# Moving layer one's twelve integer adds from VectorE to GpSimd, and ten early score products from ScalarE and GpSimd to VectorE

## The chip, the cores and the metric

The kernel runs on one core of a Trainium2 chip. The metric is device time in microseconds (us) for one execution; lower is better. A core has TensorE (PE in the profile; its weight loads are PEld), VectorE (DVE), ScalarE (ACT), GpSimd (POOL) and SyncE (SP), which here issues all DMA transfers. Each engine works through its own queue in order and waits on semaphores for the others.

## What is computed

The reference runs a chunked linear attention and then two feed-forward layers over its 3072 rows, all in fp32:

```python
# attention, per batch and head, chunk by chunk (768 positions, head_dim 32, d_state 16)
cum = np.cumsum(la, axis=-1)                          # la = log(clip(a))
L = np.exp(cum[..., :, None] - cum[..., None, :]) * causal
M = np.einsum('bhin,bhjn->bhij', Cc, Bc) * L          # scores times decays
y = einsum(M, xc) + einsum(Cc, state) * np.exp(cum)
state = decay_full * state + sum(Bx * decay_from_j)
...
# layer one: d_model 256, d_ff 768
h = np.maximum(np.maximum(x @ w1, x @ w2), x @ w3);  x = h @ w_out
# layer two: d_model 256, d_ff 1536
gate = 1 / (1 + exp(-(x @ w_gate)));  x = (gate * (x @ w_val)) @ w_out
```

The weights of both layers arrive as 64-bit floats, seen as pairs of 32-bit words, so the kernel itself turns them into fp32 and splits each into a high and a low part. Every large product is then three matmuls: low times high, high times low, high times high.

## The kernel before

**Attention.** There are 64 steps k, 8 for each of 8 chunks of 96 positions. A step makes scores on TensorE into a PSUM tile `s` (L331 for the first 16 steps, in fp32; L334 later, in bf16). It multiplies them by the decays `dec` into the SBUF tile `mt`, and TensorE multiplies `mt` with `xs` into `y` (L352). Which engine forms the product depends on k: odd steps, and all of the first four, use one VectorE multiply straight from PSUM (L346); even steps from k = 4 on use a ScalarE copy out of PSUM (L342) and then a GpSimd multiply in SBUF (L343), since GpSimd here works only on SBUF. In every step GpSimd writes a further 64 columns of `mt` (L339). `mt` is a ring of five buffers. `dec` tiles, one for two steps, are a ring of four: SyncE loads the next (L268) once the products that read an old one are done, and VectorE scans it (L290, twice a tile). After every fourth step ScalarE and VectorE split `y` into `xt_hi` and `xt_lo` (L361, L363) and VectorE transposes the state into the next chunk's `xs` (L367).

**Layer one's weights.** They come as 12 pieces, `a00`, `a01`, `a10`, ... `a51`: a block m of 128 hidden columns has a piece m0 (first two up matrices) and m1 (third up matrix, and the down matrix). SyncE loads a piece (L149), some of them queued behind a `dec` load. Decoding it takes these instructions, each over 128 x 512 words: ScalarE L164, L169, L173; VectorE L177 (shift and or into `t_a`); VectorE L182, the exact 32-bit integer add into `r_a`, which appears in the profile as a custom operation over 128 x 1024 halves of 16 bits; ScalarE L210 (the high part of `w_a`); GpSimd L212 (the low part of `w_a`). Layer two's weights go through the same function later, with the add on VectorE too.

**Feed-forward.** The 3072 rows are 6 tiles of 512. For a tile and a block m, TensorE makes three `u` tiles of six matmuls each (L401 to L403), and the larger of the three is taken by a ScalarE copy (L469) and two VectorE operations (L471, L473); ScalarE and GpSimd split it (L462, L464), and six matmuls into `o` follow. `u_0_5_0` is tile 0, block 5, first matrix. All `s` and `u` tiles share one ring of three PSUM buffers (`psu`), so a `u` or an `s` can start only when the tile three before it has been read out. Attention steps 12 to 23 are woven into tile 0.

**Order.** Python code emits the steps through small pipelines, and a scheduler then sets the order on each engine; so an edit moves rows elsewhere too.

```python
            dve.tensor_tensor(out=r, in0=t, in1=r, op=ALU.add)          # L182, in decode()
...
        if k >= 4 and k % 2 == 0:                                        # L341, in attention()
```

Of the kernel before, what the change touches and what calls it, by code (L numbers as in the profile page):

```python
# [15 lines left out]
ALU = mybir.AluOpType  # L16
# [25 lines left out]
START = 12  # L42
FIRST = 2 * NG
MASKED = 8
LEAD = 2
MTS = 5
DECS = 4
# [23 lines left out]
def scan_attention_then_ffn(ctx: ExitStack, tc: tile.TileContext, xh, ah, bch, pick, bn, w1, w2, w3,  # L71
                            wo1, wg, wv, wo2, out):
    nc = tc.nc
    act, dve, pool, pe, sp = nc.scalar, nc.vector, nc.gpsimd, nc.tensor, nc.sync
# [41 lines left out]
    def store2(wpool, tags, name):  # L116

        nb = 4 if name[0] == "d" else 7
        if len(tags) == 1:
            w = wpool.tile([128, 2, nb, 128], F32R, tag=tags[0], name=f"w_{name}")  # L120
            hi, lo = w[:, 0], w[:, 1]
        else:
            hi, lo = (wpool.tile([128, nb, 128], F32R, tag=g, name=f"w_{name}{k}")
                      for k, g in enumerate(tags))
        wt2[name] = [(hi[:, b], lo[:, b]) for b in range(nb)]
        return hi, lo
# [25 lines left out]
    def decode(raw, wpool, blocks, name):  # L152
        nb = raw.shape[1]
        second = name[0] != "a"

        def behind(k):
            return tc.issue_after(evict[k].ins) if second else ExitStack()

        f1 = raw[..., 1]
        r = stp.tile([128, DEC // 128, 128], I32, tag="r", bufs=3, name=f"r_{name}")[:, 0:nb]  # L160
        sg = sgs[len(blocks_done) % len(sgs)][:, 0:nb]
        blocks_done.append(name)
        with behind(0):
            act.activation(out=sg.bitcast(F16).rearrange("p b (n t) -> p b n t", t=2)[..., 1], in_=f1.bitcast(F32),  # L164
                           func=AF.Identity, scale=2.0 ** -112)
        if second:
            yield
        with behind(0):
            act.mul(f1.bitcast(F32), f1.bitcast(F32), 2.0 ** -112)  # L169
        if second:  # L170
            yield
        with behind(0):
            act.mul(r, raw[..., 0].bitcast(U32), 2.0 ** -29)  # L173
        yield
        t = stp.tile([128, DEC // 128, 128], I32, tag="t", bufs=2, name=f"t_{name}")[:, 0:nb]
        with behind(1):
            dve.scalar_tensor_tensor(out=t, in0=f1, scalar=3, in1=sg, op0=ALU.logical_shift_left,  # L177
                                     op1=ALU.bitwise_or)
        if second:
            yield  # L180
        with behind(1):
            dve.tensor_tensor(out=r, in0=t, in1=r, op=ALU.add)  # L182
        yield
        if second:
            hi, lo = store2(wpool, blocks, name)
            parts = [(r.bitcast(F32), slice(0, 4))]
            if name[0] != "d":
                v = r.bitcast(F32)
                q = wq[0].tile([128, 3, 128], F32, tag="q", name=f"q_{name}")
                for k, (out, x, y, op) in enumerate(((q[:, 0], v[:, 1], v[:, 3], ALU.add),  # L190
                                                     (q[:, 2], v[:, 0], v[:, 1], ALU.subtract),
                                                     (q[:, 1], q[:, 0], v[:, 0], ALU.subtract),
                                                     (v[:, 1], v[:, 2], q[:, 1], ALU.subtract))):
                    with behind(1):
                        dve.tensor_tensor(out=out, in0=x, in1=y, op=op)
                    if k % 2:
                        yield
                parts.append((q, slice(4, 7)))
            for x, at in parts:
                with behind(0):  # L200
                    act.copy(hi[:, at], x)
                yield
            for x, at in parts:
                with behind(1):
                    dve.tensor_tensor(out=lo[:, at], in0=x, in1=hi[:, at].bitcast(F32),
                                      op=ALU.subtract)
            return
        w = wpool.tile([128, 2, nb, 128], F32R, tag=name, name=f"w_{name}")
        blocks += [(w[:, 0, b], w[:, 1, b]) for b in range(nb)]
        act.copy(w[:, 0], r.bitcast(F32))  # L210
        yield
        pool.tensor_tensor(out=w[:, 1], in0=r.bitcast(F32), in1=w[:, 0].bitcast(F32),  # L212
                           op=ALU.subtract)
# [36 lines left out]
    flat = y1.rearrange("p k n -> p (k n)")  # L250
    cm = flat[:, 0:MASKED * 4 * CH].rearrange("p (k q i) -> p k q i", k=MASKED, q=4)
    bcf = [flat[:, MASKED * 4 * CH + (BW + 384) * k:][:, 0:BW + 384] for k in range(2)]
    pk = acon.tile([128, NG], F32, name="pk")
# [66 lines left out]
    def attention(k, ahead):  # L320

        c, g = steps[k]
        m = mt[k % MTS]
        if k < FIRST:
            ck = cm[:, k % MASKED]
            act.mul(ck.rearrange("p q i -> p (q i)"), bcf[c][:, BW:], pk[:, g:g + 1])
        ps = psu.tile([128, 4, 128], F32, tag="up", name=f"s{c}_{g}")
        for q in range(4):
            u = 4 * g + q
            if k < FIRST:  # L330
                pe.matmul(ps[:, q, 0:CH], bcf[c][:, 128 * q:128 * q + 128], ck[:, q],  # L331
                          start=True, stop=True)
            else:
                pe.matmul(ps[:, q, 0:CH], bi[c % 2][:, u, :], cs[c][:, u, :],  # L334
                          start=True, stop=True)
        for _ in range(ahead + 1):
            yield
        dc = dec[k // 2][:, 4 * (g % 2):4 * (g % 2) + 4]
        pool.tensor_tensor(out=m[:, :, CH:CH + N], in0=bx[c][:, 4 * g:4 * g + 4, :],  # L339
                           in1=dc[:, :, CH:LW].to_broadcast([128, 4, N]), op=ALU.mult)  # L340
        if k >= 4 and k % 2 == 0:  # L341
            act.copy(m[:, :, 0:CH], ps[:, :, 0:CH])  # L342
            pool.tensor_tensor(out=m[:, :, 0:CH], in0=m[:, :, 0:CH], in1=dc[:, :, 1:LW],  # L343
                               op=ALU.mult)
        else:
            last[0] = dve.tensor_tensor(out=m[:, :, 0:CH], in0=ps[:, :, 0:CH], in1=dc[:, :, 1:LW],  # L346
                                        op=ALU.mult)
        prepare(k)
        yield
        y = ys[g // 4]  # L350
        for q in range(4):
            pe.matmul(y[32 * q:32 * q + 32, g % 4, 0:CH + N], xs[c][:, 4 * g + q, :], m[:, q, :],  # L352
                      start=True, stop=True)
        if g % 4 == 3:
            yield
            h = g // 4
            o = (c * CP + 2 * CH * h) % RING
            src = y[:, :, 0:CH].rearrange("p (b k) i -> p b k i", k=KD)
            hi, lo = (v[:, :, o:o + 2 * CH].rearrange("p k (b i) -> p b k i", b=2)
                      for v in (xt_hi, xt_lo))  # L360
            act.copy(hi, src)  # L361
            yield
            dve.tensor_tensor(out=lo, in0=src, in1=hi.bitcast(F32), op=ALU.subtract)  # L363
            if c + 1 < NC:
                for q in range(4):
                    rows = slice(32 * q, 32 * q + 32)
                    dve.transpose(  # L367
                        out=xs[c + 1][rows, 16 * h:16 * h + 16, :].rearrange(
                            "p (g q) d -> p g q d", q=4)[:, :, q, :],
                        in_=y[rows, :, CH:128])  # L370

    def prepare(k):

        c, g = divmod(k, NG)
        if g == 0 and 0 < c < NC - 1:
            load_x(c + 1)
            splits.append(split_bc(c + 1))
        if splits and next(splits[0], None) is splits:
            splits.pop()
        n = k // 2  # L380
        if k % 2 == 0:
            if 5 <= n + 4 < NC * NP:
                load_decay(n + 4, ad)
        elif k < 9:
            decay(n + 1, n == 0)
        else:
            for i in ([n + 1] if k == 9 else []) + [n + 2]:
                if i < NC * NP:
                    with tc.issue_after(last[0].ins) if k > FIRST else ExitStack():
                        decay(i)  # L390

    def att_step(ahead=0):
        pipe.add(attention(done[0], ahead))
        done[0] += 1
# [120 lines left out]
    for k in range(START + 6):  # L515
        if k < START:
            att_step(LEAD)
        if k == 4:
# [130 lines left out]
    for p in range(NTT // 2):  # L649
        for j in range(M2 // 2):  # L650
# [6 lines left out]
            for u, step in enumerate(PLAN):  # L657
# [8 lines left out]
                else:  # L666
                    kind, i = step[0], int(step[1])
                    k = two[kind].multiply(i)
                    if kind == "v" and k is not None:
# [7 lines left out]
                                          op=ALU.subtract)  # L677
# [76 lines left out]
```

## Time and profile before

| what | value |
|---|---|
| time, median of 3 runs | 562.12 us (560.5 to 563.05) |
| the profiled execution | 562.02 us, of which the span of its instructions is 560.2 us |
| PE / PEld busy share of the span | 96% / 77% |
| DVE / ACT / POOL busy share | 70% / 58% / 22% |
| POOL busy by 40 slices | all of it in the first 17 slices (some 230 us) |

A busy PE is not a PE at its peak, since matmuls are pipelined and overlap in the profile: a 128 x 512 matmul is shown with about 390 ns, and the next one starts some 230 ns later. So PE's losses are read from starts and waits. Shares over the whole span are means over stages: GpSimd is used only up to about 230 us, and VectorE is loaded most in the first 85 us and again in layer two.

### The profile page before, as it was taken

The numbers are of one execution on the slowest core, as the hardware profiler recorded it, in microseconds if no ns is written. First come the engines' busy times: TensorE is split into PE (matmuls) and PEld (weight loads), VectorE is DVE, ScalarE is ACT, GpSimd is POOL, SyncE is SP. The second block draws the span as 40 slices with busy tenths as digits, with TensorE's granted clock in tenths as the row PEclk, the third lists the DMA queues.
The fourth block names the chain that finished last, engine by engine and source line by source line (L and its number), as shares of the span: only waits on it lengthen the run. The fifth ranks groups of instructions, "written<-read, shape, count | busy, mean of one in ns | idle before, by whom it ended". The sixth has DMA issues, their size and how long they took to land.

```text
span 560.2 us, 7934 instructions
## 1 busy us (share of the span) xinstructions
PE 539.3 (96%) x2885; PEld 428.7 (77%) x2885; DVE 391.0 (70%) x650; ACT 325.7 (58%) x580; POOL 123.7 (22%) x159
## 2 busy tenths in 40 slices
PE   5989799999999999999999999999999999999996
PEld 5867567767777778888888878877888877888884
DVE  4879986676785834699988896686455567545555
ACT  5777654343435223588698886575455565555553
POOL 3557965564655441000000000000000000000000
PEclk9999899999999999999999999999999999999999
DMA  7999885995887309104220000001000002000002
GB/s 242 343 293 245 203 174 107 196 176 127 179 219 123 64 1 332 43 13 139 75 76 0 1 1 1 0 5 71 1 0 2 0 0 76 0 1 0 1 0 76
DMA packets 32007, 50.52 MB, mean 90 GB/s; under 512 B 3168, under 2 KB 17888, under 8 KB 31968
## 3 DMA queue, kind: packets, MB, share of 16 engines
q1 hardware_dynamic: 31968, 50.02, 34.3%
q8 instruction: 22, 0.36, 0.3%
q14 instruction: 17, 0.14, 0.1%
HBM read 38.51 MB, written 3.25 MB: 75 GB/s over the span
## 4 chain that ended last, share of the span: by engine, by line
PE 80%; DMA 8%; DVE 7%; ACT 2%; issue 1%; SPq 1%; DVEq 0%; ACTq 0%
PE o L636 17%; PE ug L607 15%; PE uv L607 15%; PE u L401 8%; PE u L402 7%; PE u L403 7%; DMA raw_a<-in_w 3%; PE o L401 3%; PE o L402 3%; PE o L403 3%; DMA dec<-ad 2%; PE y L352 2%; DVE dec L290 1%; PE s L334 1%; DMA cs<-parts 1%
## 5 line engine op out<-in xcount | busy, mean ns | idle before, releaser
L636 PE MATMUL o<-hi,w_d 128*128 128x512 f32 x288 | 97.6, 390 | 0.0
L401 PE MATMUL u<-xt_hi,w_a 128*128 128x512 f32 x216 | 88.9, 412 | 2.8 <-DVE s L473 2.0
L607 PE MATMUL ug<-xt_hi,w_g 128*128 128x512 f32 x252 | 91.2, 391 | 0.0
L607 PE MATMUL uv<-xt_hi,w_v 128*128 128x512 f32 x252 | 90.1, 390 | 0.0
L402 PE MATMUL u<-xt_lo,w_a 128*128 128x512 f32 x216 | 85.9, 398 | 0.1
L403 PE MATMUL u<-xt_hi,w_a 128*128 128x512 f32 x216 | 85.5, 396 | 0.0
L636 PEld LDWEIGHTS o<-hi,w_d 128*128 128x128 f32 x288 | 53.9, 188 | 11.5 <-ACT hi L675 0.5
L676 DVE TENSOR_TENSOR lo<-y,hi 128x512 fp32r<-128x512 f32 x72 | 49.6, 688 | 16.3 <-ACT hi L675 15.3
L290 DVE TENSOR_TENSOR_SCAN dec<-dec,delta 128x388 f32<-128x388 f32 x64 | 57.9, 945 | 1.4 <-POOL mt L339 0.6
L636 PE MATMUL o<-lo,w_d 128*128 128x512 f32 x144 | 56.5, 392 | 1.4 <-DVE lo L676 1.4
L607 PEld LDWEIGHTS ug<-xt_hi,w_g 128*128 128x128 f32 x252 | 47.3, 188 | 11.5 <-ACT ug L609 0.9
L607 PEld LDWEIGHTS uv<-xt_hi,w_v 128*128 128x128 f32 x252 | 47.3, 188 | 10.5 <-DVE y L672 0.8
L462 ACT CAST hi<-s 128x512 fp32r<-128x512 f32 x36 | 22.3, 620 | 56.3 <-DVE s L473 55.8
L401 PEld LDWEIGHTS u<-xt_hi,w_a 128*128 128x128 f32 x216 | 41.4, 191 | 14.1 <-DVE s L473 2.3
L607 PE MATMUL ug<-xt_lo,w_g 128*128 128x512 f32 x126 | 49.1, 390 | 0.0
L607 PE MATMUL uv<-xt_lo,w_v 128*128 128x512 f32 x126 | 49.0, 389 | 0.0
L403 PEld LDWEIGHTS u<-xt_hi,w_a 128*128 128x128 f32 x216 | 41.4, 192 | 9.1
L675 ACT CAST hi<-y 128x512 fp32r<-128x512 f32 x72 | 44.5, 620 | 5.7 <-DVE y L672 5.7
L402 PEld LDWEIGHTS u<-xt_lo,w_a 128*128 128x128 f32 x216 | 41.3, 191 | 8.4 <-DVE xt_lo L363 0.6
L672 DVE TENSOR_TENSOR y<-uv,y 128x512 f32<-128x512 f32 x36 | 24.8, 688 | 32.0 <-PE uv L607 31.9
L614 DVE TENSOR_TENSOR y<-ug,y 128x512 f32<-128x512 f32 x36 | 24.9, 690 | 25.9 <-ACT y L611 18.3
L611 ACT COPY sv<-uv 128x512 f32<-128x512 f32 x36 | 21.1, 586 | 34.6 <-PE uv L607 34.5
(100 smaller groups left out, 968.9 us busy)
## 6 DMA issues: line engine op xcount, KB each, us to landing
dec<-ad SPq DMA_DIRECT2D x30, 388.0 KB, 5.7
raw_a<-in_w SPq DMA_DIRECT2D x18, 256.0 KB, 6.5
bi<-parts SPq DMA_DIRECT2D x36, 128.0 KB, 5.8
cs<-parts SPq DMA_DIRECT2D x36, 96.0 KB, 6.1
xs<-in_xh SPq DMA_DIRECT2D x6, 512.0 KB, 4.8
raw_g<-in_wg SPq DMA_DIRECT2D x6, 512.0 KB, 5.0
raw_v<-in_wv SPq DMA_DIRECT2D x6, 512.0 KB, 5.9
raw_d<-in_wo SPq DMA_DIRECT2D x6, 512.0 KB, 3.8
```

Source lines behind the costliest of these rows:

```text
L290: dve.tensor_tensor_scan(out=f, data0=f, data1=delta.rearrange("p u w -> p (u w)"), initial=0.0, op0=ALU.mult, op1=ALU.add)
L401: pe.matmul(ps, wlo, a_hi(k), start=k == 0, stop=False)
L402: pe.matmul(ps, whi, a_lo(k), start=False, stop=False)
L403: pe.matmul(ps, whi, a_hi(k), start=False, stop=k == kn - 1)
L462: act.copy(hl[0], s)
L607: pe.matmul(ps, w, x, start=new and e == 0, stop=e == 2, skip_group_check=not new)
L611: evict[0] = act.copy(self.temp(1 if i == 6 else 2), ps)
L614: evict[1] = dve.tensor_tensor(out=self.t[k], in0=ps, in1=self.t[k], op=ALU.add)
L636: pe.matmul(acc2[t][d], w, x, start=n == 1 and e == 0, stop=n == M2 and e == 2)
L672: evict[1] = dve.tensor_tensor(out=g, in0=v, in1=g, op=ALU.mult)
L675: act.copy(hl[0], g)
L676: dve.tensor_tensor(out=hl[1], in0=g, in1=hl[0].bitcast(F32), op=ALU.subtract)
```

## The change

Layer one's integer adds (twelve, one for each piece) are issued on GpSimd, as a 32-bit add over 128 x 512; layer two's stay on VectorE. The form of product with a ScalarE copy and a GpSimd multiply starts at step 24 and no longer at step 4, so the ten even steps 4 to 22 use the VectorE multiply.

```diff
+SHARED = 24
...
         with behind(1):
-            dve.tensor_tensor(out=r, in0=t, in1=r, op=ALU.add)
+            (dve if second else pool).tensor_tensor(out=r, in0=t, in1=r, op=ALU.add)
...
-        if k >= 4 and k % 2 == 0:
+        if k >= SHARED and k % 2 == 0:
             act.copy(m[:, :, 0:CH], ps[:, :, 0:CH])
             pool.tensor_tensor(out=m[:, :, 0:CH], in0=m[:, :, 0:CH], in1=dc[:, :, 1:LW],
                                op=ALU.mult)
```

The scheduler's order moves with it. Three places are shown; one line is added near the top of the file, so lines of the change are one higher. `s1_3` is the score tile of chunk 1, group 3 (step 11); `y0` and `y1` are the two attention outputs.

VectorE before, from step 11's product to the `xt_lo` that the first `u` needs:

```order
L346 TENSOR_TENSOR mt1_99<-s1_3_341,dec5_216 128x4x96
L182 ISA r_a01_416<-t_a01_422,r_a01_416 128x1024
L363 TENSOR_TENSOR xt_lo_93<-y1_104,xt_hi_92 128x2x2x96
L367 STREAM_TRANSPOSE xs1_155<-y1_104 32x4x32 x4
L177 SCALAR_TENSOR_TENSOR t_a10_432<-raw_a10_250,sg0_87 128x512
L290 SCALAR_TENSOR_TENSOR dec7_289<-dec7_289,delta_95 128x388 x2
L182 ISA r_a10_425<-t_a10_432,r_a10_425 128x1024
L363 TENSOR_TENSOR xt_lo_93<-y0_103,xt_hi_92 128x2x2x96
```

VectorE in the change, the same place:

```order
L347 TENSOR_TENSOR mt0_98<-s1_2_310,dec5_216 128x4x96
L347 TENSOR_TENSOR mt1_99<-s1_3_338,dec5_216 128x4x96
L364 TENSOR_TENSOR xt_lo_93<-y1_104,xt_hi_92 128x2x2x96
L368 STREAM_TRANSPOSE xs1_155<-y1_104 32x4x32 x4
L178 SCALAR_TENSOR_TENSOR t_a10_428<-raw_a10_249,sg0_87 128x512
L291 SCALAR_TENSOR_TENSOR dec7_287<-dec7_287,delta_95 128x388 x2
L364 TENSOR_TENSOR xt_lo_93<-y0_103,xt_hi_92 128x2x2x96
```

Two adds are gone from behind step 11's product, and step 10's product now stands ahead of it.

VectorE before, around the product of step 15 (`s1_7`), while TensorE is at blocks 0 and 1 of tile 0:

```order
L473 TENSOR_TENSOR s3_0_0_479<-u3_0_0_2_533,s3_0_0_479 128x512
L177 SCALAR_TENSOR_TENSOR t_a30_472<-raw_a30_334,sg0_87 128x512
L182 ISA r_a21_455<-t_a21_462,r_a21_455 128x1024
L182 ISA r_a30_465<-t_a30_472,r_a30_465 128x1024
L290 SCALAR_TENSOR_TENSOR dec9_383<-dec9_383,delta_95 128x388 x2
L177 SCALAR_TENSOR_TENSOR t_a31_492<-raw_a31_337,sg1_88 128x512
L346 TENSOR_TENSOR mt0_98<-s1_7_593,dec7_289 128x4x96
L471 TENSOR_TENSOR s3_0_1_571<-u3_0_1_1_598,s3_0_1_571 128x512
```

VectorE in the change, the same place:

```order
L474 TENSOR_TENSOR s3_0_0_475<-u3_0_0_2_528,s3_0_0_475 128x512
L347 TENSOR_TENSOR mt4_102<-s1_6_561,dec7_287 128x4x96
L178 SCALAR_TENSOR_TENSOR t_a30_468<-raw_a30_331,sg0_87 128x512
L347 TENSOR_TENSOR mt0_98<-s1_7_587,dec7_287 128x4x96
L178 SCALAR_TENSOR_TENSOR t_a31_488<-raw_a31_334,sg1_88 128x512
L291 SCALAR_TENSOR_TENSOR dec9_379<-dec9_379,delta_95 128x388 x2
L472 TENSOR_TENSOR s3_0_1_566<-u3_0_1_1_592,s3_0_1_566 128x512
```

Step 15's product now stands ahead of the two scans and of `t_a31`, with no add before it.

GpSimd before, in the last part of the decoding (`w_a50`, `w_a51` are the last two pieces):

```order
L343 TENSOR_TENSOR mt0_98<-mt0_98,dec10_522 128x4x96
L212 TENSOR_TENSOR w_a50_650<-r_a50_616,w_a50_650 128x512
L339 TENSOR_TENSOR mt3_101<-bx2_325,dec11_587 128x4x16
L464 TENSOR_TENSOR lo3_0_3_771<-s3_0_3_769,hi3_0_3_770 128x512
L343 TENSOR_TENSOR mt2_100<-mt2_100,dec11_587 128x4x96
L339 TENSOR_TENSOR mt4_102<-bx3_656,dec12_663 128x4x16
L339 TENSOR_TENSOR mt0_98<-bx3_656,dec12_663 128x4x16
L212 TENSOR_TENSOR w_a51_739<-r_a51_706,w_a51_739 128x512
```

GpSimd in the change, the same place:

```order
L183 TENSOR_TENSOR r_a50_610<-t_a50_626,r_a50_610 128x512
L213 TENSOR_TENSOR w_a41_577<-r_a41_547,w_a41_577 128x512
L183 TENSOR_TENSOR r_a51_699<-t_a51_716,r_a51_699 128x512
L465 TENSOR_TENSOR lo3_0_3_763<-s3_0_3_761,hi3_0_3_762 128x512
L340 TENSOR_TENSOR mt4_102<-bx3_649,dec12_656 128x4x16
L340 TENSOR_TENSOR mt0_98<-bx3_649,dec12_656 128x4x16
L213 TENSOR_TENSOR w_a50_644<-r_a50_610,w_a50_644 128x512
L340 TENSOR_TENSOR mt1_99<-bx3_649,dec13_742 128x4x16
L213 TENSOR_TENSOR w_a51_732<-r_a51_699,w_a51_732 128x512
```

All twelve adds and the split of block 3 (`lo3_0_3`) now stand ahead of `w_a50`; the multiplies of L343 are gone there. On TensorE the 64 steps' `y` products stand in 45 separate places instead of 42.

## Rows read from the trace of the kernel before

**Rows 1.** The page: chain of work that ended last, by engine.
```profile
PE 80%; DMA 8%; DVE 7%; ACT 2%; issue 1%; SPq 1%; DVEq 0%; ACTq 0%
```

**Rows 2.** Windows: length; PE, PEld, DVE, ACT, POOL busy (instructions); clock; DMA share; GB/s.
```profile
25.00:84.00 59.00, 51.96 (x353) 39.02 (x353) 54.24 (x81) 40.57 (x72) 43.08 (x45) 0.97 0.95 235
...
59.95:63.36 3.41, 3.41 (x9) 2.63 (x8) 3.41 (x5) 3.41 (x8) 3.41 (x3) 0.50 0.98 346
238.00:252.00 14.00, 14.00 (x64) 11.58 (x63) 13.02 (x26) 11.64 (x20) 0.00 (x0) 1.00 0.04 10
```

**Rows 3.** Timeline of PE: start us, duration us, instruction, idle before and releaser.
```profile
40.35 0.79 PE L402 MATMUL u<-xt_lo,w_a 128*128 128x512 f32 x1
...
57.10 0.40 PE L352 MATMUL y<-mt,xs 128*32 128x112 f32 x8 [1.49 <-DVE mt L346]
...
59.62 0.53 PE L401 MATMUL u<-xt_hi,w_a 128*128 128x512 f32 x1 [1.59 <-DVE s L473]
...
69.76 0.33 PE L334 MATMUL s<-cs,bi 96*128 96x96 bf16 x4 [0.27 <-DVE s L473]
...
75.46 0.33 PE L334 MATMUL s<-cs,bi 96*128 96x96 bf16 x4 [0.94 <-DVE s L471]
...
83.84 0.50 PE L401 MATMUL u<-xt_hi,w_a 128*128 128x512 f32 x1
```

**Rows 4.** Timeline of DVE, ahead of two of these PE waits.
```profile
33.43 0.56 DVE L346 TENSOR_TENSOR mt<-s,dec 128x384 f32<-128x384 f32 x1 [2.30 <-PE s L331]
33.90 0.68 DVE L182 CUSTOM_DVE_ANT_0 r_a<-t_a,r_a 128x1024 uint16<-128x1024 uint16 x1
...
39.16 0.67 DVE L182 CUSTOM_DVE_ANT_0 r_a<-t_a,r_a 128x1024 uint16<-128x1024 uint16 x1
39.74 0.55 DVE L363 TENSOR_TENSOR xt_lo<-y,xt_hi 128x384 fp32r<-128x384 f32 x1
...
50.25 3.13 DVE L182 CUSTOM_DVE_ANT_0 r_a<-t_a,r_a 128x1024 uint16<-128x1024 uint16 x2
...
55.03 1.55 DVE L177 SCALAR_TENSOR_TENSOR t_a<-raw_a,sg 128x512 int32<-128x512 int32 x1
56.50 0.55 DVE L346 TENSOR_TENSOR mt<-s,dec 128x384 f32<-128x384 f32 x1
```

**Rows 5.** Waits of the SP queue, 0 to 110 us: total us, times, longest.
```profile
SPq L268 <- DVE mt L346: 24.1, 7, 6.5
```

**Rows 6.** Groups of DVE by line, 25 to 84 us: busy, mean ns, idle before.
```profile
L182 DVE CUSTOM_DVE_ANT_0 r_a<-t_a,r_a 128x1024 uint16<-128x1024 uint16 x12 | 13.1, 1094 | 0.8 <-ACT raw_a L169 0.5
L177 DVE SCALAR_TENSOR_TENSOR t_a<-raw_a,sg 128x512 int32<-128x512 int32 x12 | 12.3, 1023 | 1.4 <-ACT raw_a L169 1.4
L346 DVE TENSOR_TENSOR mt<-s,dec 128x384 f32<-128x384 f32 x8 | 4.4, 549 | 2.3 <-PE s L331 2.3
```

**Rows 7.** Instructions on three tiles: duration ns min/median/max, first and last start.
```profile
L177 DVE SCALAR_TENSOR_TENSOR t_a<-raw_a,sg x12: 681/908/1647, 24.9 to 77.3; 128x512 int32<-128x512 int32 x12
L182 DVE CUSTOM_DVE_ANT_0 r_a<-t_a,r_a x12: 665/926/2174, 29.4 to 81.9; 128x1024 uint16<-128x1024 uint16 x12
L346 DVE TENSOR_TENSOR mt<-s,dec x14: 528/548/558, 13.8 to 98.7; 128x384 f32<-128x384 f32 x14
```

**Rows 8.** Busy time by window up to the end of `w_a50`.
```profile
25.00:76.90 51.90, 44.91 (x302) 34.35 (x302) 47.64 (x68) 37.83 (x67) 39.46 (x40) 0.97 1.01 247
```

**Rows 9.** Groups of POOL by line, 25 to 76.9 us.
```profile
L212 POOL TENSOR_TENSOR w_a<-r_a,w_a 128x512 fp32r<-128x512 f32 x11 | 15.7, 1434 | 3.7 <-ACT w_a L210 3.7
L343 POOL TENSOR_TENSOR mt<-mt,dec 128x384 f32<-128x384 f32 x8 | 9.7, 1217 | 0.0
L311 POOL TENSOR_TENSOR bc<-bc,parts 128x896 f32<-128x896 f32 x3 | 6.6, 2209 | 1.2 <-ACT parts L302 1.2
L464 POOL TENSOR_TENSOR lo<-s,hi 128x512 fp32r<-128x512 f32 x3 | 4.3, 1443 | 0.0
```

**Rows 10.** Timeline of POOL: the low part of piece a50.
```profile
75.59 1.31 POOL L212 TENSOR_TENSOR w_a<-r_a,w_a 128x512 fp32r<-128x512 f32 x1 [1.33 <-ACT w_a L210]
```

## The prediction

> **What bounds the kernel now.** I read the chain that ended last first: 80% of it is TensorE [rows 1]. The window in layer two shows what a saturated stretch looks like: 64 matmuls in 14 us, one each 0.22 us, and GpSimd unused [rows 2]. There nothing that this change touches can matter. So the question is how much TensorE loses while tile 0 runs beside layer one's decoding. Between 25 and 84 us VectorE is busy 54.2 of 59 us, 92%, and GpSimd 43.1, 73% [rows 2]. TensorE's waits there name VectorE: its `y` at 57.10 waited 1.49 us for a VectorE product, `u_0_2_0` at 59.62 waited 1.59 us for a VectorE maximum, and at 69.76 and 75.46 two score tiles waited 0.27 and 0.94 us [rows 3]. Behind the pair of waits near 57 to 59 us the granted clock is 0.50, the 1.2 GHz level, from 59.95 to 63.36 us [rows 2]. And the stream of `u` matmuls really begins at 40.35, with the first that reads `xt_lo` [rows 3], which VectorE made at 39.74 [rows 4].
>
> Why VectorE is late near 57 us stands in its timeline: step 15's product ran at 56.50, behind two adds of 3.13 us together, two scans, and a `t_a` of 1.55 [rows 4]. The product is also what SyncE waits for: its queue stood 24.1 us behind VectorE products before it could load a `dec` tile, 6.5 us at the longest [rows 5], and weight pieces are queued behind these loads. So VectorE, in this stage, is the bound.
>
> **What the change costs and gives, engine by engine.** VectorE loses twelve adds, 13.1 us, mean 1.09 [rows 6]. It gains ten products; eight of them fall into the same stretch, at 0.549 each [rows 6] that is 4.4 us. Net 54.2 - 13.1 + 4.4 = 45.5 us, if `t_a` stays as it is. Both `t_a` and the add are 0.67 to 0.68 at their fastest and up to 1.65 and 2.17, while a product that reads PSUM never leaves 0.528 to 0.558 [rows 7]. So operations with two SBUF inputs stretch beside GpSimd and those from PSUM don't: the new products are safe, and the twelve `t_a` that remain are not.
>
> The Trainium skill gives the mechanism (SBUF — State Buffer, "SBUF: two separate sides"): GpSimd and a VectorE operation with two SBUF inputs contend for a shared pair of ports, held as an exclusive lock for a whole instruction. The spread of `t_a` agrees with that; a time comes from it only in the second rival.
>
> ScalarE loses ten copies; it isn't waited for here, so I count nothing. If that cover is wrong it is a gain, since it feeds both VectorE and GpSimd.
>
> GpSimd gains twelve adds and loses ten multiplies. No row shows a 32-bit integer add on GpSimd. The nearest is the subtraction of the same size with two SBUF inputs, 1.43 us [rows 9], and I take that. From below, a gain against it can't be excluded: its fastest examples take about 1.3 [rows 10]. From above, VectorE does the add as 1024 halves; if GpSimd needed as many elements, the 896-wide subtraction of 2.21 us [rows 9] scaled by 1024/896 gives 2.52.
>
> What must be kept is the date of the weights. `w_a50` was done at 75.59 + 1.31 = 76.9 [rows 10], and `u_0_5_0` read it at 83.84 [rows 3]: 6.9 us of slack. Up to 76.9, from 25, GpSimd worked 39.5 of 51.9 us and waited 12.4 [rows 8]. In the change, up to the same instruction: 39.5, plus twelve adds (the order puts all of them ahead) at 1.43 = 17.2, minus eight multiplies, 9.7 [rows 9], plus `lo3_0_3`, now ahead as well, 1.4 [rows 9]. That is 48.4 us of work. With no waits `w_a50` would be ready at 73.4; with all the old waits at 85.8. With twelve more instructions in a queue a waited-for input is more often there already; of the waits ahead of L212, 3.7 us [rows 9], most ended on an add that VectorE had delayed. I take half of the 12.4, and get 25 + 48.4 + 6.2 = 79.6.
>
> **The sum.** (a) The start of the `u` stream: between step 11's product at 33.43, which waits for TensorE in either order, and `xt_lo` at 39.74, two adds of 0.6 each leave the queue [rows 4]: -1.2. (b) The two waits of 1.49 and 1.59 [rows 3]: step 15's product loses the adds and, by the order, the scans ahead of it: -3.1. (c) The half clock behind them, 3.41 us at half speed [rows 2]: -1.7, as TensorE no longer pauses. (d) Of the 0.27 and 0.94 [rows 3] I take half, as products have been added there: -0.6. Together -6.6 us: what VectorE gives back. With that `u_0_5_0` would come at 83.84 - 6.6 = 77.2, but its weights come at 79.6: +2.4 is given back to GpSimd. The order splits `y` in three more places; the first matmul behind a `y` takes 0.50 at 83.84 [rows 3], against the 0.39 that the section on the profile gives for one: 3 x 0.11 = +0.3. Sum: -6.6 + 2.4 + 0.3 = -3.9. From the profiled execution's 562.02 (the span of 560.2 and 1.8 around it) that is **558.1 us**. That execution lies 0.1 us from the median of the three runs, so no correction is made.
>
> The pieces' arrival isn't the limit: SyncE's wait of 6.5 us ended with step 15's product, which is now earlier, so `a50` and `a51` are loaded earlier too. If that product stayed where it is, (b) and (c) would fail and 4.8 us with them.
>
> A rule speaks against the change. The Trainium skill (GPSIMD Engine Reference, "Performance versus the Vector engine") measures a GpSimd elementwise add of two inputs at about twice VectorE's time and advises VectorE for such work. The rows bear out the ratio at 512 columns, 1.43 against 0.67 uncontended. By the rule alone the sum would be 12 x 0.76 = 9 us longer; by the rows the 1.43 lies on an engine with 12.4 us of waits to fill.
>
> **The rivals.** *Bigger gain.* GpSimd's waits shrink to 3.8 us or less, `w_a50` comes by 77.2, nothing is given back: -6.6 + 0.3 = -6.3, 555.7, and with the rest of (d) 555.1. For it: VectorE was what GpSimd mostly waited for. Against: steps' `mt` buffers still make it wait. Chance 0.14.
>
> *Lock and waits take it back, no change.* With GpSimd busier (48.4 of the 51.9 us instead of 39.5) each `t_a` may wait out most of a GpSimd operation: 0.68 + half of 1.43 = 1.4 instead of 1.02, 12 x 0.38 = 4.6 us back on VectorE, of the 8.7 given. And if GpSimd keeps all its old waits, `w_a50` comes at 85.8: 2.0 late, +0.3, 564.3. Between half and all of the waits lie 560 to 564. Chance 0.20.
>
> *A dear integer add, slower.* Every 0.1 us on the add moves `w_a50` by 1.2. It decides the sign at 1.43 + (83.84 - 0.3 - 79.6)/12 = 1.76 us, and at 1.99 the kernel is slower by over 0.5%. At 2.2: 12 x 0.77 = 9.2, `w_a50` at 88.8, +5.0 + 0.3: 567.3. At 2.52: 92.7, +8.9 + 0.3: 571.2. For it: VectorE needs a special two-halves form. Against: the same shape, operands and engine take 1.43 as a subtraction. Chance 0.16.
>
> The Trainium skill (GPSIMD Engine Reference, "Engine selection", on the exact integer add) says that GpSimd's cores add integers natively; no run here shows it yet.
>
> **How the numbers follow.** The forecast's case has 0.50, and its own range is 555.9 to 560.5 (waits of 4 to 8.5 us kept). The four cases together: a chance of being faster by over 0.5% (2.8 us, below 559.3; about what a measurement of this kernel can tell from no change) of 0.14 plus four fifths of 0.50, 0.54; slower by over 0.5% (above 564.9) 0.16 and a little of the second rival, 0.19; the rest, 0.27, within. The range that leaves out no more than 2 in 10 runs from 553.5, the bigger gain with a little more on later waits, to 565.0, the second rival's end with some way into the third.
>
> **What would show it.** In the profile after: L183 on GpSimd near 1.43 (right) or above 1.8 (third rival); `t_a` near 1.0 or near 1.4; step 15's product near 50 us and no half clock near 60 us (b, c); the first `u` with `xt_lo` near 39 us (a); `w_a50` near 79.6, and whether `u_0_5_0` waits for GpSimd; GpSimd waiting 6 us on the way there. TensorE from some 90 us on should do the same work in the same time. The forecast is wrong if waits of TensorE merely change their name from VectorE to GpSimd, or if the half clock comes back behind a new pause.

## The result and the profile after

The changed kernel takes **556.58 us** (median of 6 runs, 555.48 to 558.07); the kernel before, beside it, 561.53 (6 runs, 560.48 to 563.13). The ratio is 0.991, 95% interval 0.9895 to 0.993: faster by 3.9 to 5.9 us. A second set of 6 runs (the run "e8" below) gave 557.27 against 561.73, 0.9925 (0.990 to 0.995). The forecast was 558.1, 3.9 us less than the profiled execution of before; measured is some 4.5 to 5. The first profiled execution took 555.48 us, of which the span is 553.7. In the changed kernel the line numbers are one higher.

The windows of the changed kernel, with the columns of [rows 2]:

```profile
25.00:84.00 59.00, 51.16 (x347) 37.05 (x346) 50.30 (x85) 38.35 (x66) 49.40 (x50) 0.88 0.92 247
56.00:70.00 14.00, 12.10 (x90) 7.83 (x88) 13.83 (x25) 9.66 (x16) 14.00 (x14) 1.00 1.02 255
...
25.00:77.74 52.74, 45.61 (x324) 32.81 (x323) 47.20 (x78) 36.94 (x64) 46.39 (x47) 0.87 0.97 259
...
27.60:41.25 13.65, 10.47 (x59) 8.56 (x60) 11.56 (x19) 9.40 (x17) 9.37 (x10) 0.50 1.02 278
...
41.25:84.00 42.75, 40.02 (x277) 28.16 (x276) 36.21 (x60) 26.35 (x45) 37.67 (x37) 1.00 0.88 230
```

Against [rows 2], VectorE went from 54.2 to 50.3 us of the 59 and GpSimd from 43.1 to 49.4. There is now a stretch, 56 to 70 us, in which both are full: 13.8 and 14.0 of 14. From 41.25 to 84 us the clock is 1.00 throughout: the half clock of 59.95 to 63.36 is gone.

The places of [rows 3], timeline of PE of the changed kernel:

```profile
37.32 0.79 PE L403 MATMUL u<-xt_lo,w_a 128*128 128x512 f32 x1 [0.51 <-DVE xt_lo L364]
...
53.79 0.39 PE L402 MATMUL u<-xt_hi,w_a 128*128 128x512 f32 x1
...
60.13 0.33 PE L335 MATMUL s<-cs,bi 96*128 96x96 bf16 x4 [0.33 <-DVE s L472]
...
66.40 0.40 PE L353 MATMUL y<-mt,xs 128*32 128x112 f32 x8 [0.32 <-DVE mt L347]
...
70.12 0.47 PE L402 MATMUL u<-xt_hi,w_a 128*128 128x512 f32 x1 [1.38 <-DVE s L474]
...
79.23 0.73 PE L402 MATMUL o<-hi,w_a 128*128 128x512 f32 x2 [0.71 <-ACT hi L463]
79.80 0.40 PE L402 MATMUL u<-xt_hi,w_a 128*128 128x512 f32 x1
```

The first `u` with `xt_lo` starts 3.0 us earlier (40.35 before), `u_0_2_0` at 53.79 instead of 59.62, without a wait. The four waits shown from 60 us on are all that are left between 41 and 90: 2.74 us, where before has 4.61 (the 4.29 of [rows 3] and one of 0.32 at 48.06). `u_0_5_0`, the last row, starts at 79.80 (83.84) and waits for nothing. Some 2 us of these leads belong to the clock that TensorE had before 42 us and not to the change; e8 below shows how.

VectorE's timeline at the places of [rows 4], and two rows that show a collision:

```profile
31.61 0.56 DVE L347 TENSOR_TENSOR mt<-s,dec 128x384 f32<-128x384 f32 x1 [0.65 <-PE s L332]
...
36.74 0.53 DVE L364 TENSOR_TENSOR xt_lo<-y,xt_hi 128x384 fp32r<-128x384 f32 x1
...
48.47 0.54 DVE L347 TENSOR_TENSOR mt<-s,dec 128x384 f32<-128x384 f32 x1
...
60.46 1.85 DVE L178 SCALAR_TENSOR_TENSOR t_a<-raw_a,sg 128x512 int32<-128x512 int32 x1
```

From step 11's product to `xt_lo` the way is 5.13 us; in [rows 4] it was 6.31. Step 15's product runs at 48.47 instead of 56.50. GpSimd's timeline at that collision, and the low parts of `a50` and `a51`:

```profile
59.86 1.89 POOL L312 TENSOR_TENSOR bc<-bc,parts 128x896 f32<-128x896 f32 x1
61.72 0.75 POOL L340 TENSOR_TENSOR mt<-bx,dec 128x64 f32<-128x64 f32 x1
...
76.46 1.28 POOL L213 TENSOR_TENSOR w_a<-r_a,w_a 128x512 fp32r<-128x512 f32 x1
...
77.96 1.28 POOL L213 TENSOR_TENSOR w_a<-r_a,w_a 128x512 fp32r<-128x512 f32 x1
```

`w_a50` is done at 77.74. Groups of POOL by line, 25 us to that moment (compare [rows 9]):

```profile
L183 POOL TENSOR_TENSOR r_a<-t_a,r_a 128x512 int32<-128x512 int32 x12 | 16.3, 1360 | 2.8 <-DVE t_a L178 2.8
L213 POOL TENSOR_TENSOR w_a<-r_a,w_a 128x512 fp32r<-128x512 f32 x11 | 15.1, 1372 | 0.2 <-DMA cs<-parts 0.2
L340 POOL TENSOR_TENSOR mt<-bx,dec 128x64 f32<-128x64 f32 x18 | 7.3, 415 | 3.4 <-DVE dec L291 2.0 <-DMA raw_a<-in_w 1.0 <-PE y L353 0.4
```

The exact 32-bit add takes what the subtraction of the same size takes: 1.36 against 1.37 us. GpSimd's waits up to here are 2.8 + 0.2 + 3.4 = 6.4 us of 52.7.

How much of the lead survives is read at the start of layer two. The first `ug` matmul, in the timeline of PE of before:

```profile
279.15 0.39 PE L607 MATMUL ug<-xt_hi,w_g 128*128 128x512 f32 x1
```

and of the changed kernel:

```profile
273.56 0.39 PE L608 MATMUL ug<-xt_hi,w_g 128*128 128x512 f32 x1
```

The lead was 59.62 - 53.79 = 5.8 us at `u_0_2_0`, and is 5.6 here. The spans differ by 6.5, and the last 0.9 us doesn't come from layer two's matmuls. The last VectorE copy of the output, in before and in the change:

```profile
555.47 0.69 DVE L429 COPY y<-o 128x512 f32<-128x512 f32 x1 [0.68 <-PE o L636]
```

```profile
549.87 0.69 DVE L430 COPY y<-o 128x512 f32<-128x512 f32 x1 [0.68 <-PE o L637]
```

The lead is still 5.6 there. From that start to the end of the span, where the last output is stored, it is 4.7 us in before (4.6 in e7) and 3.8 to 4.0 in the change and in every other altered kernel below. Why is open.

### The profile page after: what moved, and what is told of

Its sections match the earlier page's. It is cut to its first block, busy times and chain, and to the rows that moved or that the text cites. A ratio compares the mean times of both kernels' runs of the same rounds, so it can differ in the third digit from the quotient of the medians.

```text
span 553.7 us, 7933 instructions
## 1 busy us (share of the span) xinstructions
PE 529.6 (96%) x2885; PEld 420.3 (76%) x2885; DVE 384.3 (69%) x648; ACT 322.1 (58%) x570; POOL 127.4 (23%) x161
## 4 chain that ended last, share of the span: by engine, by line
PE 81%; DMA 8%; DVE 6%; ACT 2%; issue 1%; SPq 1%; POOL 0%; DVEq 0%; ACTq 0%
PE o L637 17%; PE ug L608 15%; PE uv L608 15%; PE u L402 8%; PE u L404 8%; PE u L403 8%; DMA raw_a<-in_wo 3%; PE o L402 3%; PE o L403 3%; PE o L404 3%; DMA raw_a<-in_w 2%; PE y L353 2%; PE s L335 1%; DVE dec L291 1%; DMA bc<-in_bch 1%
## 5 line engine op out<-in xcount | busy, mean ns | idle before, releaser
L402 PEld LDWEIGHTS u<-xt_hi,w_a 128*128 128x128 f32 x216 | 41.1, 190 | 13.5 <-issue 4.1
L676 ACT CAST hi<-y 128x512 fp32r<-128x512 f32 x72 | 44.6, 621 | 6.1 <-DVE y L673 6.1
L404 PEld LDWEIGHTS u<-xt_hi,w_a 128*128 128x128 f32 x216 | 41.1, 190 | 9.2 <-issue 0.2
L403 PEld LDWEIGHTS u<-xt_lo,w_a 128*128 128x128 f32 x216 | 41.1, 191 | 8.8 <-DVE xt_lo L364 1.0
L472 DVE TENSOR_TENSOR s<-u,s 128x512 f32<-128x512 f32 x36 | 24.7, 687 | 25.5 <-PE u L404 23.3
```

The lines of the kernel that those rows point to most:

```text
L402: pe.matmul(ps, wlo, a_hi(k), start=k == 0, stop=False)
L403: pe.matmul(ps, whi, a_lo(k), start=False, stop=False)
L404: pe.matmul(ps, whi, a_hi(k), start=False, stop=k == kn - 1)
L472: dve.tensor_tensor(out=s, in0=banks[1], in1=s, op=ALU.max)
L676: act.copy(hl[0], g)
```

## Experiments

Three theories went into the runs. **First**: VectorE was the bound; taking the adds off it is the relief, and dropping GpSimd's multiplies is what lets GpSimd carry them in time. So each half alone should fail. **Second**: the gain is only the shorter way of a score product, one VectorE instruction instead of a ScalarE and a GpSimd one. **Third**: some 2 us of spread between runs of one kernel, and part of the first profile's lead, come from the clock that TensorE happens to have in the first 40 us or so.

**e1: the adds alone.** The multiplies of steps 4 to 22 go back to ScalarE and GpSimd.

```diff
-SHARED = 24
+SHARED = 4
```

> Only the twelve adds move to GpSimd; the ten products keep their ScalarE copy and GpSimd multiply. Theory 1 (VectorE was the bound; the adds are the relief, and the removed multiplies are what keeps GpSimd on time): step 15's product comes early and the half clock near 60 us is gone, but GpSimd has 58 us of work up to w_a50 instead of 48, w_a50 is ready only near 85 us, TensorE waits for GpSimd ahead of it, and the time is 559 to 563 us, at least half of the change's gain of 5 us lost. Theory 2 (the gain is the shorter way of a product, one operation instead of copy and multiply): no gain without it, 561 to 562 us, with TensorE waiting for products made by GpSimd.

563.23 us (12 runs), ratio to before 1.0036 (1.0016 to 1.0056): slower, and just above the expected 559 to 563. Its window and its timeline of PE:

```profile
25.00:84.00 59.00, 44.51 (x327) 32.79 (x326) 44.59 (x70) 39.40 (x70) 54.59 (x57) 0.86 0.87 226
```

```profile
38.12 0.77 PE L402 MATMUL u<-xt_hi,w_a 128*128 128x512 f32 x1 [4.38 <-POOL mt L340]
...
66.17 0.47 PE L402 MATMUL u<-xt_hi,w_a 128*128 128x512 f32 x1 [2.98 <-ACT mt L343]
```

VectorE drops to 44.6 us (without the products the forecast's terms give 54.2 - 13.1 = 41.1), but GpSimd is at 54.6 of 59 and TensorE now waits for it: 4.4 us for columns of `mt`. The wait of 2.98 is a PSUM buffer held by a ScalarE copy of a score.

**e2: the products alone.** All adds back on VectorE, products as in the change.

```diff
-            (dve if second else pool).tensor_tensor(out=r, in0=t, in1=r, op=ALU.add)
+            dve.tensor_tensor(out=r, in0=t, in1=r, op=ALU.add)
```

> Only the ten products move to VectorE; the adds stay there too. Theory 1: VectorE's work from 25 to 84 us rises by 4.4 to some 58.6 of 59 us, so TensorE's waits for VectorE grow: 563 to 567 us, slower than before. Theory 2: the shorter way of a product brings most of the gain by itself, 557 to 559 us.

566.6 us (5 runs), 1.0086 (1.0066 to 1.0105): slower by 4 to 5 us. The second theory falls, as the shorter way alone brings no gain. Windows, one wait of PE, and the instructions on two tiles:

```profile
25.00:84.00 59.00, 45.60 (x295) 32.20 (x296) 52.76 (x88) 38.29 (x65) 33.90 (x36) 0.83 0.96 236
...
80.25:83.66 3.41, 3.41 (x15) 2.05 (x15) 2.30 (x4) 0.91 (x2) 1.83 (x3) 0.50 0.39 117
```

```profile
79.97 0.59 PE L402 MATMUL u<-xt_hi,w_a 128*128 128x512 f32 x1 [2.67 <-DVE s L474]
```

```profile
L178 DVE SCALAR_TENSOR_TENSOR t_a<-raw_a,sg x12: 677/700/1021, 25.8 to 75.6; 128x512 int32<-128x512 int32 x12
...
L183 DVE CUSTOM_DVE_ANT_0 r_a<-t_a,r_a x12: 666/687/2008, 28.6 to 76.8; 128x1024 uint16<-128x1024 uint16 x12
```

GpSimd is idle for 25 us, VectorE (at 52.8 us, not the expected 58.6) is late again, and a wait of 2.67 us is followed by a half clock. With GpSimd that idle, `t_a` and the add have medians of 0.70 and 0.69, where [rows 7] show 0.91 and 0.93.

**e3: a dearer add.** Useless work for GpSimd ahead of each of the twelve adds; the output doesn't change.

```diff
+        if not second:
+            junk = acon.tile([128, 2, 128], I32, tag="junk", name=f"junk_{name}")
+            pool.tensor_tensor(out=junk, in0=t[:, 0:2], in1=r[:, 0:2], op=ALU.add)
```

> The changed kernel with a second, useless integer add of half the size (128 x 256) on GpSimd before each of the twelve, so that an add costs about 1.36 + 0.7 = 2.05 us. This prices GpSimd's slack. If GpSimd's queue is nearly the limit (w_a50 ended 2.1 us before its first use): eleven or twelve times 0.7 us make w_a50 some 5 to 8 us later, 4 to 6 us of it reach TensorE, 560 to 563 us. Rival: the queue has room for it, since GpSimd still waits several microseconds there: under 558 us.

564.95 us (7 runs), 1.0057 (1.0034 to 1.0079): above the expected 560 to 563. Each extra add took 0.73 us as the instruction is shown, 8.8 in all; the kernel lost 564.95 - 556.58 = 8.4 by the medians. Work added to GpSimd in the changed kernel costs about its own length. Two waits of TensorE, and the windows of the half clocks behind them:

```profile
67.21 0.50 PE L405 MATMUL u<-xt_hi,w_a 128*128 128x512 f32 x1 [0.69 <-POOL w_a L216]
...
87.80 0.73 PE L405 MATMUL o<-hi,w_a 128*128 128x512 f32 x2 [2.48 <-ACT hi L466]
```

```profile
67.92:71.34 3.42, 3.42 (x13) 2.41 (x12) 1.77 (x2) 2.35 (x4) 3.42 (x6) 0.50 1.07 184
88.41:91.82 3.41, 3.41 (x10) 2.64 (x9) 0.00 (x0) 1.15 (x2) 2.39 (x2) 0.50 0.01 6
```

The first stands behind three waits close together, 0.73 at 64.53, 0.86 at 65.79 and the 0.69 shown. Each of the two half clocks costs some 1.7 us as an estimate (3.4 us at half speed), so about 3.4 of the 8.4 are the clock and the rest is waiting.

**e4: TensorE kept busy at the start.** Twelve useless matmuls on zeros into a `psu` buffer.

```diff
+    warm = psu.tile([128, 512], F32, tag="up", name="warm")
+    for _ in range(12):
+        pe.matmul(warm, sgs[1].bitcast(BF16)[:, 0, 0:128],
+                  sgs[1].rearrange("p b n -> p (b n)").bitcast(BF16)[:, 0:512], start=True, stop=True)
```

> The changed kernel with twelve useless 128x512 bf16 matmuls on zeros at the start, while TensorE waits for its first data. Theory 3 (runs of either kernel differ by some 2 us by whether TensorE's clock rises to 2.4 GHz during the first score steps or only near 42 us): the clock rises early in every run, the fp32 score steps 0 to 11 end 1.7 us or more earlier than 33.3 us, and the runs lie together at 553 to 556 us, none at 557.5 to 558. Rival (the early steps are bound by VectorE, transfers and weight loads, and the spread has another cause): same two groups of times as the changed kernel, 555.5 to 558.

561.12 us (12 runs, 554.13 to 562.75), 0.997: a failed experiment. The extra buffer changed the scheduler's order (the first `u` waited 4.49 us for `w_a`), and in its profile a step's eight score matmuls take 2.02 us again from 14 us on. So it says nothing on the third theory.

**e5: the last two adds back on VectorE.** If GpSimd's date for `a50` and `a51` were the only thing left, this would gain.

```diff
-            (dve if second else pool).tensor_tensor(out=r, in0=t, in1=r, op=ALU.add)
+            (dve if second or name in ("a50", "a51") else pool).tensor_tensor(out=r, in0=t, in1=r, op=ALU.add)
```

> The changed kernel with the adds of the last two pieces, a50 and a51, back on VectorE (which is busy only 8.5 of 14 us from 70 to 84 us). GpSimd loses 2.6 us right ahead of w_a50. If GpSimd's queue sets the date at which tile 0 ends (the dear add cost nearly its whole extra time): 1 to 2.5 us faster than the changed kernel, 554 to 555.7 us. If GpSimd only sets it once its queue is lengthened, and VectorE and ScalarE set it in the changed kernel (its waits name VectorE's maximum and ScalarE's split, none names GpSimd): within 1 us of the changed kernel, 555.7 to 557.6.

559.88 us (12 runs), 0.995 (0.993 to 0.997), some 3 us more than the change by the medians. PE's timeline and the window behind it:

```profile
74.42 0.79 PE L402 MATMUL u<-xt_hi,w_a 128*128 128x512 f32 x1 [1.91 <-DVE s L474]
```

```profile
74.07:77.49 3.42, 3.07 (x14) 2.02 (x14) 3.42 (x6) 1.56 (x3) 3.42 (x4) 0.50 0.44 128
```

The wait that is 1.38 us in the change is 1.91 here, and the half clock is back. So VectorE has no room for two adds either. Half of these runs, the profiled one among them, have the early half clock that e8 tells of; against runs of the change of the same kind the loss is 0.9 us (557.4 and 556.5) and 2.3 us (560.0 and 557.7).

**e6: the switch at step 16 and at step 32.**

```diff
-SHARED = 24
+SHARED = 16
```

> The changed kernel with the VectorE products only up to step 15: four even steps, 16 to 22, go back to copy and multiply. GpSimd gets 4 x 1.2 = 4.8 us more up to the end of the decoding, VectorE loses 2.2. Theory 1 (the products' part is there to keep GpSimd on time): 558 to 561 us. If what the products bring is only the early start of tile 0 (steps 8 to 14): within 1 us of the changed kernel.

559.93 us (12 runs), 0.9972 (0.9956 to 0.9987), as the first theory had it. One of the two waits shown now names GpSimd, and the larger one ScalarE:

```profile
65.84 0.50 PE L402 MATMUL u<-xt_hi,w_a 128*128 128x512 f32 x1 [0.75 <-POOL w_a L213]
...
72.60 0.95 PE L402 MATMUL o<-hi,w_a 128*128 128x512 f32 x2 [1.95 <-ACT hi L463]
```

With 32 instead:

> The changed kernel with the VectorE products up to step 31, so four more even steps of tile 1, where VectorE is busy about 9 of 14 us and the decoding is over. Theory 1: nothing is bound there by either engine, so within 1 us of the changed kernel, 555.5 to 557.5. If a product made in one operation is worth something by itself: 0.5 us or more faster for each pair, 554 to 555.5.

559.52 us (12 runs, 557.65 to 564.61), 0.9972 (0.9948 to 0.9995): a miss, no better and more scattered. Its waits up to 84 us are those of the change, so where it loses is open.

**e7: before once more, for a profile.**

> The kernel before once more, for a second profile. The profile at hand shows 2.02 us for the eight matmuls of a score step before 40 us; the changed kernel's shows 1.10. If this is a difference of TensorE's clock between executions and not the change's doing, this kernel too shows 1.10 in some of its executions, with a time near 560.5 to 561.2 and a mean clock near 0.98, and 2.02 in those near 562 to 563 with a clock of 0.995. If the change makes it, 2.02 here again, whatever the time.

562.84 us, with the same half clock near 60 us; the other early clock didn't turn up.

**e8: the change once more.**

> The changed kernel once more, unaltered. If the two groups of times come from TensorE's early clock (third theory), the runs fall near 555.5 to 556.7 and near 557.5 to 558.3, each some 4.7 us under the group of before with the same mean clock, and the median ratio lies between 0.988 and 0.994. If the difference of 5 us was partly luck of which runs fell into which group, the ratio comes out above 0.994.

557.27 us (6 runs, 555.79 to 559.76), ratio 0.9925: the gain is confirmed, and the ratio lies where the third theory had it. Timeline of PE, eight score matmuls of a step in before, in the change, and in e8 at two times; then e8's first `u` with `xt_lo`:

```profile
21.76 2.02 PE L331 MATMUL s<-y 128*128 128x96 f32 x8
```

```profile
21.88 1.13 PE L332 MATMUL s<-y 128*128 128x96 f32 x8
```

```profile
14.73 1.13 PE L332 MATMUL s<-y 128*128 128x96 f32 x8
...
21.75 2.02 PE L332 MATMUL s<-y 128*128 128x96 f32 x8
...
38.02 0.80 PE L403 MATMUL u<-xt_lo,w_a 128*128 128x512 f32 x1 [1.40 <-DVE xt_lo L364]
```

A window of e8, and one of before:

```profile
20.56:34.22 13.66, 12.25 (x100) 9.75 (x99) 12.03 (x22) 11.15 (x19) 9.87 (x12) 0.50 1.06 292
```

```profile
20.00:25.00 5.00, 5.00 (x35) 4.00 (x33) 4.13 (x6) 3.99 (x8) 3.77 (x4) 1.00 1.06 290
```

There are two kinds of execution. In before and in e7 a step's eight score matmuls take 2.02 us, half rate, in every step from 14 us to 33. In the change and in e8 they take 1.13 us, full rate, at 14 us, and a half clock of some 13.7 us comes later: from 27.60 in the change, from 20.56 in e8. So e8 is of the change's kind; its half clock coming 7 us earlier moved the first `u` with `xt_lo` by 0.7 us and the span by 0.3. What half rate from the start costs is read from e6 at 32, whose profile is of before's kind and whose waits up to 84 us are the change's:

```profile
22.30 2.02 PE L332 MATMUL s<-y 128*128 128x96 f32 x8
...
39.61 0.79 PE L403 MATMUL u<-xt_lo,w_a 128*128 128x512 f32 x1
...
56.00 0.39 PE L402 MATMUL u<-xt_hi,w_a 128*128 128x512 f32 x1
...
72.33 0.47 PE L402 MATMUL u<-xt_hi,w_a 128*128 128x512 f32 x1 [1.39 <-DVE s L474]
```

Its `u_0_2_0`, the third row, comes 2.2 us behind the change's 53.79, and at 72.33 it is still 2.2 behind. So about 2 of the 6.5 us between the first two profiles are the early clock, as the third theory had it.

The times agree. In the profiles (e4's aside) an execution's mean granted clock tells the kind: 0.993 or more where half rate lasts from the start, 0.991 or less where full rate comes first. Taken for all runs, this puts 39 runs of before (those beside e1, e5 and e8) in the second kind with a median of 561.2 us and 26 in the first with 562.5; of the change's 12 runs, 7 have 556.5 and 5 have 557.7. Like with like, the change gains 4.7 and 4.8 us. For a run without a profile the kind is inferred from its mean clock, not seen.

**e9: the last two subtractions on VectorE** (adds stay on GpSimd).

```diff
-        pool.tensor_tensor(out=w[:, 1], in0=r.bitcast(F32), in1=w[:, 0].bitcast(F32),
+        (dve if name in ("a50", "a51") else pool).tensor_tensor(out=w[:, 1], in0=r.bitcast(F32), in1=w[:, 0].bitcast(F32),
```

> The changed kernel with the two subtractions of pieces a50 and a51 on VectorE instead of GpSimd; all adds stay on GpSimd. If GpSimd alone sets the date of the last two pieces (the recorded reason for the 2.4 us given back), w_a50 and w_a51 come 1.4 to 2.7 us earlier than 77.7 and 79.2 us and the time falls by 0.7 to 2 us, to 554 to 556. If the two engines are balanced there (what moving the two adds back suggested), the time is that of the changed kernel or up to 2 us more, 556.5 to 558.5, with TensorE's waits naming VectorE near 70 to 80 us.

555.52 us (6 runs, 555.23 to 557.35), 0.9896 (0.9875 to 0.9917). Beside e8, on the same chip, it is 1.75 us less by the medians, but the intervals overlap, and by mean clock five of its six runs have the full rate first, three of e8's (such runs: 555.5 against the change's 556.5). VectorE's timeline, then PE's:

```profile
74.26 1.56 DVE L213 TENSOR_TENSOR w_a<-r_a,w_a 128x512 fp32r<-128x512 f32 x1 [1.15 <-ACT w_a L211]
...
79.11 0.67 DVE L213 TENSOR_TENSOR w_a<-r_a,w_a 128x512 fp32r<-128x512 f32 x1
```

```profile
53.91 0.51 PE L335 MATMUL s<-cs,bi 96*128 96x96 bf16 x8 [0.92 <-DMA cs<-parts]
...
70.62 0.47 PE L402 MATMUL u<-xt_hi,w_a 128*128 128x512 f32 x1 [1.34 <-DVE s L474]
...
77.48 0.39 PE L402 MATMUL u<-xt_hi,w_a 128*128 128x512 f32 x1
```

`w_a50` is ready at 74.26 + 1.56 = 75.8, 1.9 earlier, the wait of 0.71 at 79 us is gone, and `u_0_5_0` (last row) runs 2.3 earlier, in part because the order puts less work ahead of it. But a DMA wait of 0.92 us is new, and its span equals the change's, 553.7. It is at least as fast as the change; that it is faster is likely and not settled.

## Why the prediction was right, and where its terms were off

**The bound.** Right: VectorE's lateness was what TensorE paid for. e1 and e2 show that this needs both halves: each alone is slower, by 0.4% and 0.9%, and together they gain 0.9%. The forecast treated the products as 4.4 us of cost to VectorE; it didn't say that they pay for the adds' place on GpSimd, but its GpSimd sum holds that term (8 multiplies, 9.7 us), and e1 and e6 at 16 show it in the times. VectorE's 45.5 us became 50.3: `t_a` grew by 1.1, and with TensorE further along some 3.8 us more of scans, transposes, maxima and `xt_lo` falls into the same window.

**(a) -1.2.** Right: 6.31 to 5.13 us between product and `xt_lo`. The start moved by 3.0 (2.3 in e8), since step 11's product itself ran at 31.61 instead of 33.43, but that part is the early clock. In e6 at 32, with before's early clock, the first `u` with `xt_lo` comes at 39.61: 0.7 us earlier than in before, 1.6 earlier than in e7 (41.23).

**(b) -3.1 and (c) -1.7.** Right: both waits and the half clock are gone. At `u_0_2_0`, which both orders reach with the same work done, the lead is 5.8, of which 2.2 is the early clock; of the 3.6 that remain (59.62 against 56.00 in e6 at 32) 0.7 is the start, so (b) brought 2.9. From there `u_0_3_1` comes after 9.64 us, at 63.43, where before needed 10.61, to 70.23. The stretch has one run of `y` (0.3 us) more and a wait of 0.33, before's has the wait of 0.27: 10.61 - 9.64 + 0.3 + 0.33 - 0.27 = 1.3 for (c), somewhat less than forecast.

**(d) -0.6.** This step failed in sign. Half of 1.21 us was to go; waits of 2.74 stand there now. The largest, 1.38 at 70.12, is a score or `u` buffer that VectorE hadn't read out, at the end of the stretch in which VectorE is busy 13.83 of 14 us. The prediction warned that products were added there and still counted half a gain; TensorE also gets there 6.5 us earlier (76.62 in before), and VectorE, full in that stretch, doesn't keep up.

**+2.4 to GpSimd.** The date was well worked out: 48.4 us of work and 6.2 of waits were forecast up to `w_a50`, 46.4 and 6.4 measured, so 79.6 became 77.74. The work is 2.0 less mostly because three kinds of operation came cheaper: 1.36 for the add and 1.37 for the subtraction instead of 1.43, 1.29 instead of 1.44 for the split into `lo`. But the reason for the loss failed: no wait names `w_a50`. TensorE lost its time at 70.12 to VectorE and at 79.23 to the ScalarE split of `hi`, two of the waits counted under (d), and so came to `u_0_5_0` when the weights lay ready. That they make 2.1 us together, close to the 2.4, is luck. The weights were only 2.1 us ahead, and e3's price, 8.4 us for 8.8 of added work, shows how little that is.

**The price of the add.** The third rival is dead: 1.36 us, nowhere near 1.76. The Trainium skill (GPSIMD Engine Reference, "Engine selection") says that the cores add integers natively, and the trace agrees: the 32-bit add and the fp32 subtraction differ by 12 ns over these stretches.

**The lock.** Of the second rival a little came true: `t_a` has a mean of 1.12 us instead of 1.02, 12 x 0.09 = 1.1 us, where the rival had 4.6. The pair at 60 us shows how: `t_a` was issued at 60.46, inside GpSimd's `bc` operation that ended at 61.75, and ended 0.56 us behind that; GpSimd's next, at 61.72, took 0.75 for work that takes 0.30 alone, since it ended just behind `t_a` in turn. The Trainium skill (SBUF — State Buffer, "SBUF: two separate sides") calls this an exclusive lock held for a whole instruction; these rows and e2's short medians agree with it.

**The size.** The forecast of -3.9 was 0.6 to 1 us short of the medians, 0.8 to 0.9 short like with like. The two profiles give 6.5, of which 2.2 is the early clock. The rest up to the first `ug`, with e6 at 32 for the start: 0.7 + 2.9, 1.0 between `u_0_2_0` and `u_0_3_1`, less the 1.2 by which the lead shrinks from there (6.8 to 5.6): 3.4 us, or 4.2 against e7. The forecast's 3.9 is a sum for this part, and it came out about right, but in part by luck, since what (d) had wrong in sign was booked as a loss to GpSimd that didn't come. The 0.7 to 0.9 us behind the last output copy is in none of its terms.

**Open.** Runs of one kernel spread over 2 to 4 us (in e8's set: before 560.4 to 563.4, the change 555.8 to 559.8). The kind of early clock accounts for 1.2 to 1.4 of it by the medians above; what decides the kind isn't shown, and e4 failed to force it. No run changes the engines at an unchanged order, so what the new order brings by itself isn't separated from what the moved work brings.

## What to carry to other kernels

When one engine is the bound of a stage, moving work off it pays only as far as the receiver has idle time ahead of its own due dates; free that time in the same edit, and test each half alone: here each lost. Price the receiver by its dates (work plus waits up to the instruction that someone waits for), and count the waits that the earlier arrival of TensorE will open on the old bound. A wait of a microsecond or two of TensorE may cost as much again through its clock: look for both in the rows. Before subtracting two profiles, compare the duration of an early instruction that the change doesn't touch: here the two were not of one kind, and 2 us of the difference was not the change.

## What the runs showed of the hardware

- The clock column can't be trusted ahead of a record's first change. In before, eight score matmuls take 2.02 us near 22 us in a window that is shown with a clock of 1.00; in e8, with the same 2.02, the window is shown with 0.50. Until the first change in a record the durations tell the clock, not the column.
- Half rate from the start up to some 42 us (e6 at 32) put `u_0_2_0` 2.2 us behind an execution that had full rate first and 13.65 us of half clock later (the change), with the same waits from 42 to 84 us in both. When that later stretch lies costs little: beginning 7 us earlier (e8) it moved the span by 0.3, with TensorE's own waits there shifting too (3.91 us for a VectorE product at 29.58 in the change, 1.41 at 30.69 in e8).
- Waits of 1.91 us (e5), 2.67 (e2) and 2.48 (e3) of TensorE stand next to a half clock of 3.4 us; the 1.38 us at 70.12 in the change, and the 1.34 in e9, don't. e3's other half clock stands behind three shorter ones, 0.73, 0.86 and 0.69 within 3 us, so the length of a single wait doesn't decide.
